# Downsampled and local attention feeding a SiLU layer: q and k on the two partition halves, 18 transposes for each early pair, later landings in the planner, paced loads

## The chip, the cores and the metric

The kernel runs on one core of a Trainium2 chip. The metric is the device time in microseconds (us) of one execution. Engines are named as in the profile: PE is the matmul engine (PEld its weight loads), DVE, ACT and POOL are the vector, scalar and GpSimd engines, SP issues DMAs.

## The reference, cut to what matters

Inputs are q, k and v of shape 8 x 8 x 576 x 64 (batch, heads, sequence, head width) and two weight matrices, 512 x 2048 and 2048 x 512, all float32.

```python
def _attn_ref(q, k, v):
    q_d = q.reshape(B, H, Sd, 4, D).mean(axis=3)      # k_d, v_d likewise, Sd = 144
    out_up = np.repeat(sm_attn(q_d, k_d, v_d), 4, axis=2)
    mask = np.abs(pos[:, None] - pos[None, :]) < 4
    scores = np.where(mask, scale * np.matmul(q, k.transpose(0, 1, 3, 2)), -1e9)
    ...
    return out_up + np.matmul(attn, v)                # attn: softmax of scores

x = attn_out.transpose(0, 2, 1, 3).reshape(B * S, H * D)   # 4608 x 512
h = x @ w_in                                               # 4608 x 2048
out = (h * (1.0 / (1.0 + np.exp(-h)))) @ w_out             # 4608 x 512
```

So there are two attentions for each head, one over sequence elements averaged by four and one in a band of seven, whose sum is the input of a two-layer network.

## The kernel before, in words

Two heads make a pair; there are 32 pairs, four to a batch. For a pair p the stages are:

- **Loads** (`load_qk`, `load_v`, `load_vq`): q and k go into one of four buffers `qk`, v into `vs` (four 64-partition DMAs) and, from pair 14 on, into `vq`. SP issues nearly all of them (L464 is the helper that issues every DMA). A partition of `qk` holds nine sequence rows of one head. The q load fills 128 partitions with both heads of pair p. The k load starts one head later, so it holds the second head of pair p and the first head of pair p+1; the first head of pair 0 is fetched alone, through `Rb`, by `lkx` and cast by `ckx`.
- **Casts** (`cast`, L535 to L544; `castw`, L551 and L554; `castv`): to bf16, on DVE and ACT for pairs 0 and 1 and on POOL later. `qkb` has NB = 3 buffers.
- **Transposes** (`pe_T`, L572): 36 of 64 x 64 for a pair, q into the PSUM bank `o0` and k into `pe_`, in an order that visits the four quadrants of the PE array in turn. `after_T` evacuates them to `qT` (L362) and `kT` (L582) and sums groups of four into `qd` and `kd` (L586, L590, and L597/L599 on POOL for pairs 0 to 7).
- **S** (`pe_S`): banded and downsampled scores into the banks `AB`; `after_S` takes exponentials on ACT (L624, L626) and applies the band mask on DVE (L628).
- **Z and PV** (`pe_main`): softmax sums and the products with v, into `CD` (for pairs 1 and 3 into `HP`). The reciprocals are spread over `Rb`, for pairs 0 to 9 by ten matmuls (`RB`, L735; the three-part split of the reciprocal is L707 to L714) and later through a DRAM scratch.
- `after_PV` multiplies (L745) and POOL adds the two attentions into `xT` (L769).
- **g1 and g2**: the first layer runs in 144 groups of four float32r matmuls into one of two `HP` banks, then tanh on ACT (L783) and a product on DVE into `gT` (L785). The second layer runs in 144 groups of four bf16 matmuls into `o0` or `pe_`; ACT evacuates (L800) and SP stores. L359 is the helper that issues all matmuls except transposes.

The program is written as units with a guessed cost each. Pairs 0 to 9 have separate units T, S, Z, PV, RB and VP; groups of g1 come in from the sixth round. From pair 10 on one unit V holds S of pair n, the transposes of pair n+1 and the rest of earlier pairs, with four g1 and four g2 parts written behind it. `feed` creates the loads and casts as far ahead as the buffers allow. `Plan.order` then simulates the five engines with the guessed costs and landing times, picks for each engine the ready unit of best priority inside a window (14 for PE), and so fixes the order of every engine's stream. At run time each engine follows that order and waits on semaphores. `tick` can make the loads of a pair wait for the exponentials of an earlier pair, from pair NTH on; with NTH = 99 it never acts. The weights (`load_w`) come in eight 1 MiB reads that POOL issues, with planned times from 16 us on.

Of the kernel before, what the change touches and what calls it, by code (L numbers as in the profile page):

```python
# [18 lines left out]
NVP = 14  # L19
NDIR = 10  # L20
NEQ = 12
NTH = 99
NMQ = 8


# [126 lines left out]
class Unit:  # L152


    __slots__ = ("eng", "name", "ops", "cost", "dcost", "prio", "idx", "pre", "succ", "npre",
                 "ready", "start", "end", "fifo")

    def __init__(self, eng, name, cost, prio, dcost=0.0):
        self.eng, self.name, self.cost, self.prio, self.dcost = eng, name, cost, prio, dcost
        self.ops, self.pre, self.succ = [], set(), []  # L160
        self.ready = 0.0


FIRST = {
# [2 lines left out]
class Plan:  # L167
# [50 lines left out]
    def order(self, look, first):  # L218

        todo = {e: first.get(e, "").split() for e in Prog.ENGS}  # L220
        free = {e: 0.0 for e in Prog.ENGS}
        ring = {e: 0.0 for e in Prog.ENGS}
        for u in self.units:
            u.pre = {v for v in u.pre}
            u.npre = len(u.pre)
            for v in u.pre:
                v.succ.append(u)
        pend = {e: [u for u in self.units if u.eng == e] for e in Prog.ENGS}
        head = {e: 0 for e in Prog.ENGS}
        taken = set()  # L230
        res = []
        left = len(self.units)
        while left:
            best = None
            for e in Prog.ENGS:
                lst = pend[e]
                while head[e] < len(lst) and lst[head[e]] in taken:
                    head[e] += 1
                if todo[e]:
                    win = [next(u for u in lst[head[e]:] if u.name == todo[e][0] and u not in taken)]  # L240
                    if win[0].npre:
                        continue
                else:
                    win = [u for u in lst[head[e]:head[e] + look[e]] if u not in taken and not u.npre]
                if not win:
                    continue
                t = max(free[e], min(u.ready for u in win))
                c = min((u for u in win if u.ready <= t + 0.05), key=lambda u: (u.ready - 100000 if u.fifo else u.prio, u.idx))
                t = max(t, c.ready)
                if best is None or t < best[0]:  # L250
                    best = (t, c)
            t, u = best
            del todo[u.eng][:1]
            u.start = t
            free[u.eng] = t + u.cost
            if u.dcost:
                e = u.eng
                begin = max(t + u.cost + 0.4, ring[e])
                other = max(x for y, x in ring.items() if y != e)
                ring[e] = begin + u.dcost + min(u.dcost, max(0.0, other - begin))  # L260
                u.end = ring[e] + (3.2 if e == "ACT" else 1.6)
                if e == "SP":
                    free[e] = max(free[e], ring[e] - 4.0)
            else:
                u.end = t + u.cost + self.LAT[u.eng]
            for v in u.succ:
                v.npre -= 1
                same = v.eng == u.eng and not u.dcost
                v.ready = max(v.ready, t + u.cost + (0.06 if u.eng != "PE" else 0.0) if same else u.end)
            taken.add(u)  # L270
            res.append(u)
            left -= 1
        res.sort(key=lambda u: u.start)
        return res


def bass_hourglass_attn__then__act_silu_kernel(
# [9 lines left out]
    with kctx:  # L287
        E = kctx.enter_context
        L = Plan()
# [20 lines left out]
        vs = sb("vs", [128, 10, 64], F32, NVS)  # L310
        vq = sb("vq", [128, 4, 256], F32, NVQ)
        vt = sb("vt", [128, 4, 128], F32)
        qkb = sb("qkb", [128, 2, 576], BF16, NB)
        vb = sb("vb", [128, 10, 64], BF16, NV)
        vd = sb("vd", [128, 4, 64], BF16, NV)
        qT = sb("qT", [128, S_], BF16, NT)
# [144 lines left out]


        def dma(eng, name, out_, in_, w, sem, dcost, r=(), prio=None, cost=0.42):
            return one(eng, name, cost, lambda s: s.dma_start(out_, in_), r, w, sem, prio, dcost)  # L464

        def tick(p, d):
            return [R(f"tick{p - d}")] if p >= NTH else []

        def load_qk(p):
            i = p % NQK  # L470
            ek = "ACT" if p < 1 else "SP"
            if p == 0:
                dma("ACT", "lkx", Rb[NR - 1][64:128, 0:576], bass.AP(tensor=k.tensor, offset=k.offset,
                                                                   ap=[[576, 64], [1, 576]]),
                    [R(f"Rb{NR - 1}1")], "kx", 0.5, prio=-20)
            dma("SP", f"lq{p}", qk[i][:, 0, :], bass.AP(tensor=q.tensor, offset=q.offset + 128 * p * 576,
                                                        ap=[[576, 128], [1, 576]]),
                [R(f"qk{i}0")], f"qk{i}0", 0.85, r=tick(p, 4), prio=10 * p)
            n = 128 if p < NPAIR - 1 else 64
            dma(ek, f"lk{p}", qk[i][0:n, 1, :], bass.AP(tensor=k.tensor, offset=k.offset + (128 * p + 64) * 576,  # L480
                                                          ap=[[576, n], [1, 576]]),
                [R(f"qk{i}1")], f"qk{i}1", 0.85, r=tick(p, 4), prio=10 * p)

        def load_v(p):
            i = p % NVS
# [45 lines left out]

        def cast(p):
            i, j = p % NQK, p % NB
            if p == 0:
                one("ACT", "ckx", 0.7, lambda e: e.activation(qkb[NB - 1][64:128, 1, :], Rb[NR - 1][64:128, 0:576],  # L535
                                                              AF.Copy),
                    r=[R(f"Rb{NR - 1}1")], w=[R(f"qkb{NB - 1}1")])
            if p < 2:
                one("DVE", f"cq{p}", 0.45, lambda e: e.tensor_copy(qkb[j][:, 0, :], qk[i][:, 0, :]),  # L539
                    r=[R(f"qk{i}0")], w=[R(f"qkb{j}0")])  # L540
                one("DVE", f"ck{p}", 0.45, lambda e: e.tensor_copy(qkb[j][:, 1, :], qk[i][:, 1, :]),  # L541
                    r=[R(f"qk{i}1")], w=[R(f"qkb{j}1")])
            else:
                one("POOL", f"c{p}", 1.15, lambda g: g.tensor_copy(qkb[j][:, :, :], qk[i][:, :, :]),  # L544
                    r=[R(f"qk{i}0"), R(f"qk{i}1")], w=[R(f"qkb{j}0"), R(f"qkb{j}1")])

        def castw(p):
            i, m = p % NVS, p % NV
# [14 lines left out]

        def pe_T(u, p):
            a, b = p % NB, (p - 1) % NB
            for r in range(9):
                for j, h, x, t, n in ((0, 0, 0, o0, a), (0, 1, 1, pe_, a), (1, 1, 0, o0, a), (1, 0, 1, pe_, b)):
                    o = t[half(h), 0:288].bitcast(BF16)[:, 64 * r:64 * r + 64]  # L570
                    w = qkb[n][half(j), x, 64 * r:64 * r + 64]
                    L.op(u, lambda e, o=o, w=w, j=j: e.transpose(o, w, idn[half(j), :]),  # L572
                         [R("id"), R(f"qkb{n}{x}")], [rE if x else rF])

        def after_T(p):
            j = p % NT
# [230 lines left out]
        def T(p):  # L807
            made.add(("T", p))
            u = L.unit("PE", f"T{p}", 0.45 if p > 1 else 0.9)
            pe_T(u, p)  # L810
            after_T(p)

        def VP(p):
# [42 lines left out]
        def feed():  # L856

            for p in range(NPAIR):
                for name, fn, need in (
                    ("lqk", load_qk, ("c", NQK)), ("c", cast, ("T", NB - 1)),  # L860
                    ("lv", load_v, ("cw", NVS)), ("cw", castw, ("PV", NV)),
                    ("lvq", load_vq, ("cv", NVQ)), ("cv", castv, ("PV", NV)),
                ):
                    src = {"c": "lqk", "cw": "lv", "cv": "lvq"}.get(name)
                    if p < NVP and name in ("lvq", "cv"):
                        made.add((name, p))
                    if (name, p) in made or (src and (src, p) not in made):
                        continue
                    if p >= NTH and name[0] == "l" and ("x", p - (4 if name == "lqk" else 3)) not in made:
                        continue  # L870
                    if p >= need[1] and (need[0], p - need[1]) not in made:
                        continue
                    if name in ("lv", "lvq") and ("lqk", p) not in made:
                        continue
                    made.add((name, p))
                    fn(p)
# [42 lines left out]
        while todo or todo2:  # L919
            if n < NPAIR + 2:  # L920
# [3 lines left out]
                if n <= NVP:  # L924
                    VP(n - 1)
                feed()
            m = 4
            G1(1 if m else 0)
            G2((0,))
            G1(1 if m else 0)  # L930
            G2((1,))
            G1(1 if m else 0)
            G2((2, 3))
            G1(m - 3 if m else 0)
            n += 1
        P = Prog()
        for u in L.order({"PE": 14, "ACT": 40, "DVE": 40, "POOL": 30, "SP": 40}, FIRST):
# [36 lines left out]
```

## Time and profile before

| | |
|---|---|
| median of 4 runs (lowest to highest) | 359.89 us (358.64 to 359.96) |
| the profiled execution: its own time, its span | 359.96 us, 358.2 us |
| PE busy | 331.3 us, 4742 matmuls |
| DVE, ACT, POOL busy | 222.5, 182.0, 156.2 us |
| matmuls of the first layer (HP) | 576, 162.6 us |
| matmuls of the second layer (o and pe_) | 576, 133.8 us |
| transposes (L572) | 1152, 33.6 us |
| moved by DMA | 60.28 MB, mean 168 GB/s |

Busy times of matmuls overlap each other and themselves, so they don't add to the span. In lines of the profile, a row gives the line of the kernel, the engine, the operation, output<-input, shapes and count, then busy us, mean ns, and the engine's idle time just ahead of such instructions with what released it. "issue" is time in which an engine waited for nothing that the profile shows.

### The profile page before, as it was taken

To read this page: it belongs to the slowest core of one execution; us is meant where nothing else is said; L and a number is where in the kernel's file an instruction comes from. 1 tells how busy PE (TensorE), PEld (TensorE's weight loads), DVE (VectorE), ACT (ScalarE), POOL (GpSimd) and SP (SyncE) were. 2 spreads that over 40 slices of the span, in tenths; PEclk is the share of its full clock that TensorE was granted. 3 is DMA by queue.
4 is the path that set the end of the run, shared out by engine and by line. 5 is a ranking of instruction groups with operands and counts; after the bars stand their busy time and mean duration, and the time that the engine had idled before them with its cause. 6 is when DMAs were issued, how large, how long until landed. Compare 5 with 4: busy or idle time off the path is not lost.

```text
span 358.2 us, 11023 instructions
## 1 busy us (share of the span) xinstructions
PE 331.3 (92%) x4742; PEld 214.6 (60%) x4742; DVE 222.5 (62%) x392; ACT 182.0 (51%) x326; POOL 156.2 (44%) x203
## 2 busy tenths in 40 slices
PE   0675599989999999999999999999999999999996
PEld 0454476667666666666666666666665565666642
DVE  7579659985666677777777767666655434343400
ACT  2855567875555555455545555555553444444421
POOL 7849774553455566655555657563111100000000
PEclk9996579999999999999999999999999999999999
DMA  8999999997998878877778775232032000110012
GB/s 234 239 277 277 292 274 238 267 228 208 234 284 235 228 218 214 233 203 225 212 226 211 215 196 161 73 119 75 33 123 95 31 29 29 42 48 29 31 59 88
DMA packets 73506, 60.28 MB, mean 168 GB/s; under 512 B 47986, under 2 KB 55794, under 8 KB 73458
## 3 DMA queue, kind: packets, MB, share of 16 engines
q1 hardware_dynamic: 63818, 44.27, 45.7%
q10 hardware_dynamic: 5416, 9.02, 8.8%
q0 software_dynamic: 4224, 6.29, 7.9%
q8 instruction: 37, 0.61, 0.7%
q14 instruction: 11, 0.09, 0.1%
HBM read 51.76 MB, written 9.91 MB: 172 GB/s over the span
## 4 chain that ended last, share of the span: by engine, by line
PE 87%; DVE 3%; SPq 2%; ACT 2%; issue 2%; POOL 1%; DMA 1%; ACTq 0%; POOLq 0%
PE HP L359 39%; PE o L359 28%; PE pe_ L359 8%; PE CD L359 6%; PE AB L359 4%; SPq L464 2%; PE o L572 2%; DMA vs<-in_v_dram 1%; DVE zr L707 1%; DVE rp L713 1%; DVE kd L586 1%; DVE rrest L711 1%; ACT Pt L624 0%; PE pe_ L572 0%; POOL w_in_sb L464 0%
## 5 line engine op out<-in xcount | busy, mean ns | idle before, releaser
L359 PE MATMUL HP<-xT,w_in_sb 128*128 128x512 f32 x576 | 162.6, 419 | 0.6 <-issue 0.5
L785 DVE SCALAR_TENSOR_TENSOR gT<-th,HP 128x512 bf16<-128x512 f32 x144 | 96.5, 683 | 101.4 <-ACT th L783 100.8
L783 ACT ACTIVATE th<-HP 128x512 f32<-128x512 f32 x144 | 86.1, 598 | 76.5 <-PE HP L359 74.3
L359 PEld LDWEIGHTS HP<-xT,w_in_sb 128*128 128x128 f32 x576 | 106.3, 190 | 27.3 <-issue 0.8
L359 PE MATMUL o<-w_out_bf,gT 128*128 128x512 bf16 x464 | 107.4, 380 | 0.1
L359 PEld LDWEIGHTS o<-w_out_bf,gT 128*128 128x128 bf16 x464 | 42.4, 98 | 54.9 <-issue 9.7
L769 POOL TENSOR_TENSOR xT<-xo 128x576 fp32r<-128x576 f32 (+3 forms) x48 | 44.1, 930 | 54.4 <-DVE xo L745 54.4
L800 ACT ACTIVATE osb<-o 128x512 f32<-128x512 f32 x29 | 17.3, 597 | 60.9 <-PE o L359 60.9
L554 POOL CAST vb<-vs 128x640 bf16<-128x640 f32 x30 | 21.8, 728 | 54.2 <-PE CD L359 41.9
L544 POOL CAST qkb<-qk 128x1152 bf16<-128x1152 f32 x30 | 34.3, 1145 | 5.4 <-DMA qk<-in_k_dram 4.6
L745 DVE TENSOR_TENSOR xo<-CD,Rb 128x720 f32<-128x720 f32 x30 | 27.0, 900 | 3.0 <-PE CD L359 1.1
L359 PE MATMUL pe_<-w_out_bf,gT 128*128 128x512 bf16 x112 | 26.4, 380 | 0.0
L559 POOL TENSOR_TENSOR vt<-vq 128x512 f32<-128x512 f32 x18 | 22.9, 1273 | 7.1 <-DMA vq<-in_v_dram 7.1
L572 PE MATMUL o<-idn,qkb 64*64 64x64 bf16 x576 | 17.2, 203 | 9.1 <-DVE qkb L539 6.3
L586 DVE TENSOR_REDUCE kd<-kT 128x144 bf16<-128x576 bf16 x32 | 23.3, 731 | 0.9 <-ACT kT L582 0.8
L582 ACT ACTIVATE kT<-pe_ 128x576 bf16<-128x576 bf16 x32 | 20.9, 654 | 1.7 <-PE pe_ L572 0.2
L624 ACT ACTIVATE Pt<-AB 128x576 bf16<-128x576 f32 x32 | 20.7, 647 | 1.5 <-PE AB L359 1.5
L572 PEld LDWEIGHTS o<-idn,qkb 64*64 64x64 bf16 x576 | 13.9, 118 | 11.0 <-DVE qkb L539 6.3
L572 PE MATMUL pe_<-idn,qkb 64*64 64x64 bf16 x576 | 16.4, 203 | 2.5 <-DVE qkb L541 1.9
L359 PEld LDWEIGHTS pe_<-w_out_bf,gT 128*128 128x128 bf16 x112 | 10.0, 98 | 13.6 <-issue 3.2
L590 DVE TENSOR_REDUCE qd<-qT 128x144 bf16<-128x576 bf16 x24 | 17.8, 744 | 0.0
L626 ACT ACTIVATE Pd<-AB 128x432 bf16<-128x432 f32 x32 | 16.9, 527 | 0.0
(79 smaller groups left out, 315.4 us busy)
## 6 DMA issues: line engine op xcount, KB each, us to landing
vs<-in_v_dram SPq DMA_DIRECT2D x126, 80.0 KB, 4.2
qk<-in_q_dram SPq DMA_DIRECT2D x32, 288.0 KB, 4.0
out_dram<-osb SPq DMA_DIRECT2D x36, 256.0 KB, 3.0
qk<-in_k_dram SPq DMA_DIRECT2D x30, 288.0 KB, 5.3
Rb<-scr ACTq DMA_DIRECT2D x44, 180.0 KB, 4.7
vq<-in_v_dram SPq DMA_DIRECT2D x18, 256.0 KB, 6.2
w_in_sb<-in_moe_w_in_dram POOLq DMA_DIRECT2D x4, 1024.0 KB, 9.4
w_out_bf<-in_moe_w_out_dram POOLq DMA_DIRECT2D x4, 512.0 KB, 9.3
```

The source lines that it names most:

```text
L359: L.op(u, lambda t: t.matmul(out_, lhsT, rhs, start=start, stop=stop, skip_group_check=True), r, w)
L544: one("POOL", f"c{p}", 1.15, lambda g: g.tensor_copy(qkb[j][:, :, :], qk[i][:, :, :]), r=[R(f"qk{i}0"), R(f"qk{i}1")], w=[R(f"qkb{j}0"), R ...
L554: one("POOL", f"cw{p}", 0.72, lambda g: g.tensor_copy(vb[m][:, :, :], vs[i][:, :, :]), r=rr, w=[R(f"vb{m}")])
L559: one("POOL", f"va{p}", 1.3, lambda g: g.tensor_tensor(vt[:, :, :], vq[i][:, :, 0:128], vq[i][:, :, 128:256], ALU.add), r=rr, w=[R("vt")])
L572: L.op(u, lambda e, o=o, w=w, j=j: e.transpose(o, w, idn[half(j), :]), [R("id"), R(f"qkb{n}{x}")], [rE if x else rF])
L582: one("ACT", f"ek{p}", 0.68, lambda e: e.activation(kT[j][:, 3:579].rearrange("p (g r) -> p g r", r=9), pe_[:, 0:288].bitcast(BF16).rearra ...
L586: one("DVE", f"mk{p}", 0.74, lambda e: e.tensor_reduce(kd[j][:, 0:SD], kT[j][:, 3:579].rearrange("p (g r) -> p g r", r=4), AX.X, ALU.add), ...
L624: one("ACT", f"x{p}", 0.66, lambda e: e.activation(Pt[m][:, :, :], AB[:, :, 0:288], AF.Exp, scale=0.125), r=rAB, w=[R(f"P{m}"), R(f"tick{p ...
L745: one("DVE", f"m{p}", 0.92, prio=-450000 if L.boost else None, r=rCD + [R(f"Rb{u}0"), R(f"Rb{u}1")], w=[R(f"xo{x}")], fn=lambda e: e.tenso ...
L769: one("POOL", f"a{p}", 0.15 + n * 0.0019, lambda g, dst=dst, in0=in0, in1=in1: g.tensor_tensor(dst, in0, in1, ALU.add), r=[R(f"xo{x}")], w ...
L783: one("ACT", f"t{j}_{f}", 0.62, lambda e: e.activation(th[tb][:, :], hps[hb], AF.Tanh, scale=0.5), r=[rH[hb]], w=[R(f"th{tb}")], prio=-1)
L785: one("DVE", f"s{j}_{f}", 0.71, lambda e: e.scalar_tensor_tensor(gT[j % 2][:, f, :], th[tb][:, :], 1.0, hps[hb], ALU.add, ALU.mult), r=[rH ...
```

## The change

- q of a pair goes to partitions 0-63 and k to partitions 64-127, both heads side by side in the free dimension; the separate fetch and cast of k's first head (`lkx`, `ckx`) disappear. The first k load stays on ACT's queue.
- `qkb` becomes [128, 9, 2, 64]: for each of the nine rows the two heads are neighbours. Casts write that order. Pair 0 is cast half on DVE, half on ACT; pair 1 in one DVE instruction; later pairs on POOL as before. A cast now needs the transposes three pairs back instead of two.
- `pe_T` takes a parameter. In the T units (pairs 0 to 10) it is wide: 18 transposes of 64 x 128. In V it stays at 36 of 64 x 64, in another order of quadrants.
- The planner assumes that SP loads with a priority number of 70 or more land 5.0 us after their transfer instead of 1.6. That is q and k from pair 7 on, `vs` from pair 6 on (later `vq` too).
- NTH is 12: from pair 12 on a q or k load waits for the exponentials of the pair four before, a v load for those of the pair three before.
- In the steady loop one g2 part is written first, then two g1, three g2 and two g1, instead of alternating.

```diff
-NTH = 99
+NTH = 12
+PLAT, LATE = 7, 5.0
...
-                u.end = ring[e] + (3.2 if e == "ACT" else 1.6)
+                u.end = ring[e] + u.lat
...
-        qkb = sb("qkb", [128, 2, 576], BF16, NB)
+        qkb = sb("qkb", [128, 9, 2, 64], BF16, NB)
...
+            u = one(eng, name, cost, lambda s: s.dma_start(out_, in_), r, w, sem, prio, dcost)
+            if eng == "SP" and prio is not None and prio >= 10 * PLAT:
+                u.lat = LATE
+            return u
...
+            for x, e, t in ((0, "SP", q), (1, ek, k)):
+                dma(e, f"l{'qk'[x]}{p}", qk[i][half(x), :, :],
+                    bass.AP(tensor=t.tensor, offset=t.offset + 2 * p * S_ * D_, ap=[[576, 64], [S_ * D_, 2], [1, 576]]),
+                    [R(f"qk{i}{x}")], f"qk{i}{x}", 0.85, r=tick(p, 4), prio=10 * p)
...
+            o, a = qkb[j][:, :, :, :].rearrange("p r h d -> p h r d"), qk[i][:, :, :].rearrange("p h (r d) -> p h r d", d=64)
+            rr = [R(f"qk{i}0"), R(f"qk{i}1")]
             if p == 0:
+                one("DVE", f"ca{p}", 0.45, lambda e: e.tensor_copy(o[:, 0], a[:, 0]), r=rr, w=[R(f"qkb{j}")])
+                one("ACT", f"cb{p}", 0.68, lambda e: e.activation(o[:, 1], a[:, 1], AF.Copy), r=rr, w=[R(f"qkb{j}")])
+            elif p < 2:
+                one("DVE", f"ca{p}", 0.85, lambda e: e.tensor_copy(o, a), r=rr, w=[R(f"qkb{j}")])
             else:
+                one("POOL", f"c{p}", 1.15, lambda g: g.tensor_copy(o, a), r=rr, w=[R(f"qkb{j}")])
...
-        def pe_T(u, p):
-            a, b = p % NB, (p - 1) % NB
+        def pe_T(u, p, wide=False):
+            b = p % NB
             for r in range(9):
-                for j, h, x, t, n in ((0, 0, 0, o0, a), (0, 1, 1, pe_, a), (1, 1, 0, o0, a), (1, 0, 1, pe_, b)):
-                    o = t[half(h), 0:288].bitcast(BF16)[:, 64 * r:64 * r + 64]
-                    w = qkb[n][half(j), x, 64 * r:64 * r + 64]
...
+                for h in range(1 if wide else 2):
+                    for x, t in ((0, o0), (1, pe_)):
+                        c = slice(0, 128) if wide else half(h)
+                        o = t[c, 0:288].bitcast(BF16)[:, 64 * r:64 * r + 64]
+                        w = qkb[b][half(x), r, :, :].rearrange("p h d -> p (h d)")[:, c]
...
-            pe_T(u, p)
+            pe_T(u, p, True)
...
-                    ("lqk", load_qk, ("c", NQK)), ("c", cast, ("T", NB - 1)),
+                    ("lqk", load_qk, ("c", NQK)), ("c", cast, ("T", NB)),
...
-            m = 4
-            G1(1 if m else 0)
             G2((0,))
-            G1(1 if m else 0)
-            G2((1,))
-            G1(1 if m else 0)
-            G2((2, 3))
-            G1(m - 3 if m else 0)
+            G1(2)
+            G2((1, 2, 3))
+            G1(2)
```

More of the change, by code (lines that the diff above doesn't have):

```diff
@@ L155 @@
     __slots__ = ("eng", "name", "ops", "cost", "dcost", "prio", "idx", "pre", "succ", "npre",
-                 "ready", "start", "end", "fifo")
+                 "ready", "start", "end", "fifo", "lat")
     def __init__(self, eng, name, cost, prio, dcost=0.0):
@@ L161, in __init__ @@
         self.ready = 0.0
+        self.lat = 3.2 if eng == "ACT" else 1.6
 FIRST = {
@@ L463, in dma @@
         def dma(eng, name, out_, in_, w, sem, dcost, r=(), prio=None, cost=0.42):
-            return one(eng, name, cost, lambda s: s.dma_start(out_, in_), r, w, sem, prio, dcost)
+            u = one(eng, name, cost, lambda s: s.dma_start(out_, in_), r, w, sem, prio, dcost)
+            if eng == "SP" and prio is not None and prio >= 10 * PLAT:
+                u.lat = LATE
+            return u
         def tick(p, d):
@@ L471, in load_qk @@
             ek = "ACT" if p < 1 else "SP"
[L472 to L482, printed above, removed]
+            for x, e, t in ((0, "SP", q), (1, ek, k)):
+                dma(e, f"l{'qk'[x]}{p}", qk[i][half(x), :, :],
+                    bass.AP(tensor=t.tensor, offset=t.offset + 2 * p * S_ * D_, ap=[[576, 64], [S_ * D_, 2], [1, 576]]),
+                    [R(f"qk{i}{x}")], f"qk{i}{x}", 0.85, r=tick(p, 4), prio=10 * p)
         def load_v(p):
@@ L533, in cast @@
             i, j = p % NQK, p % NB
+            o, a = qkb[j][:, :, :, :].rearrange("p r h d -> p h r d"), qk[i][:, :, :].rearrange("p h (r d) -> p h r d", d=64)
+            rr = [R(f"qk{i}0"), R(f"qk{i}1")]
             if p == 0:
[L535 to L542, printed above, removed]
-            else:
-                one("POOL", f"c{p}", 1.15, lambda g: g.tensor_copy(qkb[j][:, :, :], qk[i][:, :, :]),
-                    r=[R(f"qk{i}0"), R(f"qk{i}1")], w=[R(f"qkb{j}0"), R(f"qkb{j}1")])
+                one("DVE", f"ca{p}", 0.45, lambda e: e.tensor_copy(o[:, 0], a[:, 0]), r=rr, w=[R(f"qkb{j}")])
+                one("ACT", f"cb{p}", 0.68, lambda e: e.activation(o[:, 1], a[:, 1], AF.Copy), r=rr, w=[R(f"qkb{j}")])
+            elif p < 2:
+                one("DVE", f"ca{p}", 0.85, lambda e: e.tensor_copy(o, a), r=rr, w=[R(f"qkb{j}")])
+            else:
+                one("POOL", f"c{p}", 1.15, lambda g: g.tensor_copy(o, a), r=rr, w=[R(f"qkb{j}")])
         def castw(p):
@@ L562, in castv @@
                 vd[m][:, :, :], vt[:, :, 0:64], vt[:, :, 64:128], ALU.add), r=[R("vt")], w=[R(f"vd{m}0"), R(f"vd{m}1")])
-        def pe_T(u, p):
-            a, b = p % NB, (p - 1) % NB
+        def pe_T(u, p, wide=False):
+            b = p % NB
             for r in range(9):
-                for j, h, x, t, n in ((0, 0, 0, o0, a), (0, 1, 1, pe_, a), (1, 1, 0, o0, a), (1, 0, 1, pe_, b)):
-                    o = t[half(h), 0:288].bitcast(BF16)[:, 64 * r:64 * r + 64]
-                    w = qkb[n][half(j), x, 64 * r:64 * r + 64]
-                    L.op(u, lambda e, o=o, w=w, j=j: e.transpose(o, w, idn[half(j), :]),
-                         [R("id"), R(f"qkb{n}{x}")], [rE if x else rF])
+                for h in range(1 if wide else 2):
[3 more added lines that the diff above has]
+                        w = qkb[b][half(x), r, :, :].rearrange("p h d -> p (h d)")[:, c]
+                        L.op(u, lambda e, o=o, w=w, x=x: e.transpose(o, w, idn[half(x), :]),
+                             [R("id"), R(f"qkb{b}")], [rE if x else rF])
         def after_T(p):
```

## The prediction

> **What bounds the kernel now.** I read the strip of 40 slices first (each 8.96 us), with the DMA queue table.
>
> ```profile
> PE   0675599989999999999999999999999999999996
> ...
> PEclk9996579999999999999999999999999999999999
> DMA  8999999997998878877778775232032000110012
> ...
> q8 instruction: 37, 0.61, 0.7%
> ```
>
> PE is full from the ninth or tenth slice on, so from about 80 us the kernel is a queue of matmuls. Before that PE idles while the DMA engines are full, and in slices 4 to 6 it runs at about half clock. The windows view splits this:
>
> ```profile
> 50.00:60.00 10.00, 9.40 (x196) 6.57 (x189) 9.04 (x16) 8.57 (x17) 6.11 (x8) 1.00 1.16 248
> ...
> 120.00:140.00 20.00, 20.00 (x373) 13.34 (x371) 13.11 (x22) 11.02 (x20) 10.45 (x11) 1.00 0.81 219
> ```
>
> Columns: stretch, length, busy us and instructions of PE, PEld, DVE, ACT, POOL, clock, DMA share, GB/s. PE has no idle time in 120:140, nor in any stretch from 80 to 340. Idle PE is 358.2 - 331.3 = 26.9 us: 8.2 before the first transposes run (6.34 us of wait, 1.88 more), 3 at the end behind the last store, and some 15.7 in between, all before 80 us. The change can win only there, or lose anywhere.
>
> The waits view, PE alone, names part of it; the PE timeline shows where:
>
> ```profile
> PE HP L359 <- issue: 2.5, 2, 2.0
> PE AB L359 <- DVE rp L714: 2.4, 1, 2.4
> PE o L572 <- POOL qkb L544: 2.0, 3, 1.1
> ...
> PE CD L359 <- issue: 1.8, 1, 1.8
> ...
> PE AB L359 <- issue: 1.3, 1, 1.3
> ```
>
> ```profile
> 30.35 0.42 PE L359 MATMUL CD<-Pt,vb 64*64 64x58 bf16 x14 [1.83 <-issue]
> ...
> 37.64 0.36 PE L359 MATMUL HP<-Pt,vb 64*64 64x58 bf16 x9 [1.98 <-issue]
> ...
> 44.75 0.46 PE L359 MATMUL AB<-rp,gT 128*128 128x72 bf16 x5 [1.27 <-issue]
> ```
>
> Each stall cuts a run of equal matmuls in two: no operand is late. Three more windows count the matmuls between them:
>
> ```profile
> 30.30:37.60 7.30, 4.13 (x128) 3.39 (x128) 5.48 (x8) 3.46 (x7) 7.12 (x10) 0.50 1.31 289
> 37.60:44.70 7.10, 5.03 (x127) 4.12 (x128) 5.05 (x10) 3.79 (x8) 4.80 (x6) 0.50 1.27 308
> ```
>
> 128 matmuls with 128 weight loads are 256 instructions, and PE's 2 x 4742 instructions over 37 packets of queue q8 are 256.3 each. So PE waits for its own program: a block about every 7.2 us, behind a DMA system whose share is near 1.3. That costs 5.1 us (1.83 + 1.98 + 1.27).
>
> [...] In the trace four transposes start together (27.94, 27.95, 27.95, 27.95). [...]
>
> **The change part by part.**
>
> Wide transposes. 11 pairs x 18 = 198 matmuls and as many weight loads go, 1.55 blocks. By the third stall eight pairs have been transposed: 144 of 732 matmuls, so that point comes 1.1 blocks earlier in the program. Around it a pair has 123 matmuls (36 T, 28 S, 14 Z, 28 PV, 10 RB, 7 VP), then 105: a block lasts 123/105 = 1.17 times as long. The work inside the two stretches above, without their closing stall, is 7.3 - 1.98 = 5.3 and 7.1 - 1.27 = 5.8 us; times 1.17 it is 6.2 and 6.8, against 7.2 that a fetch needs. Stalls of 1.0 and 0.4 stay, say 0.6 for the first: 2.0 of 5.1, a gain of 3.1. Bounds: 0, if late loads fill the gap, and 5.1.
>
> Their own time. A narrow set took 0.54 us at half clock (40.78 to 41.32) and 0.31 at full (52.81 to 53.12). Of a wide transpose there is no row. Nearest are the ten RB matmuls of 128 x 128 with 72 columns: 0.71 us at half clock, 0.33 at full, 71 and 33 ns each. At 64 columns 18 of these are 1.14 or 0.53 us alone, half that if the two row groups overlap. So a wide set costs between 0 and 0.6 more at half clock; 8 such and 3 at full clock bound the sum at 5.4. [...] I take 0[...].
>
> First pair. `lkx` (144 KB) and `ckx` (0.68 on ACT) go; k of pair 0 is issued at 0.82 instead of 1.40 and has 0.6 us less in front (144 KB at 240 GB/s). T0 waits for the slower of the half casts (0.45 DVE, 0.68 ACT), so about 7.5 instead of 8.47. But the chain view goes at 8.74 to 12.90 through the v load of pair 1, behind SP's issues, and an ACT cast at 13.01; only the lighter queue helps it. I take 0.5, between 0 and 1.0.
>
> Casts. On POOL 1.15 us with another output order; POOL rows with three-dimensional patterns (L769, 1.22 for 576 elements) are no slower per element than plain ones (L559, 1.27 for 512), so 0; bound 0.5 x 8 pairs. DVE: 1.77 us becomes about 1.3. One pair more of room for `qkb` meets 2.0 us of PE waits on POOL casts; I take 0.5, as POOL is near full there (7.12 of 7.30).
>
> Later landings move only the planned order. POOL waited 9.3 us in five places for v before its cast, up to 2.3 each; at 42.08 that held back an `xT` addition (42.83) that HP needs. I take 0.4, between -1.5 (a cast put too late) and 1.5.
>
> Pacing adds a wait for ACT on SP from pair 12, behind which sit later loads and, from 84 us, stores. Pair 12 was loaded at 59.5 and now waits for its exponentials at about 63.5; its transposes come near 83. From there V takes 8.6 us: a load released by V(p-4) has three such rounds against a landing of 5 us. So 0; if SP stood still, `osb` has two buffers and ACT would stop after them.
>
> Steady loop: the planner already placed HP, HP, four g2, HP, HP after V, since `o0` holds transposed q until its copy is done; the new text gives the same. Narrow transposes keep four quadrants and 36 instructions. Tail unchanged: 0.
>
> New part: 3.1 + 0.5 + 0.5 + 0.4 = 4.5. Everything removed exposes the next limit: DMA share is 1.1 to 1.3 until 75 us, and loads pace POOL. I give back a quarter, 1.1, leaving 3.4. The profiled execution is 359.96 (span 358.2 and 1.8 around it), 0.07 above the median. **359.9 - 3.4 = 356.5 us.**
>
> **Rivals.** *The clock comes back earlier:* half clock ended at about 50, after the dense stretch that began at 45. HP work at half clock took 3.57 for eight matmuls against 1.85. [...]
>
> *DMA paces the start:* 8.76 MB moved from 20 to 50 us, and POOL waited for v right after. If all stalls turn into load waits, only the lighter queue, 0.5, is left: 359.4, no change.
>
> [...] each q or k load now fills 64 partitions. Rows to 64 partitions exist: 2880-byte packets into `Rb` have a median of 114 ns, 25 bytes per ns, like the 93 ns of 2304-byte q and k packets, but the upper quarter begins at 187 against 108. From 8 to 75 us there are 3137 q and k packets over 16 engines, 196 each. If a packet's mean rises by 50 ns (123 to 173), the loads need 9.8 us more; with the main gain gone too and two thirds of it exposed by full queues, 359.9 + 6.5 - 3.4 = 363.0. It decides from about 17 ns per packet, where 196 x 17 ns eats the gain.
>
> *Not what it says:* the order of the planner comes out worse (a cast waiting ahead of an addition) and wins nothing: 360 to 361, with the slower ones.
>
> **How the numbers follow.** Main case 0.42, early clock 0.16, DMA-paced 0.14[...]. About 0.3%, 1.1 us, is what a measurement of this kernel can tell from no change. Faster 0.42 + 0.16 = 0.58, same 0.14, slower 0.28. The main case alone spans 354 to 358; for 8 in 10 [...] 351 to 363. I predict 356.5.
>
> **What would show it.** Right: 4544 matmuls on PE, 35 or 36 q8 packets, "issue" waits under 2.5 us, HP starting before 45 us, PE full from under 80 us. Wrong: 2304-byte packets well over 123 ns and longer POOL waits on qk; wide sets over 0.8 us; PE idle after 80 us, with SP waiting for ACT Pt ahead of stores.

## The result, and the profile after

| | before | after |
|---|---|---|
| median over all runs (lowest to highest) | 359.84 us (358.08 to 363.08) | 362.06 us (359.86 to 365.67) |
| ratio, 95% interval | | 1.006 [1.0044, 1.0076] |
| the profiled execution: its own time, its span | 359.96, 358.2 | 362.02, 360.3 |
| PE busy, PE idle in the span | 331.3, 26.9 | 329.3, 31.0 |
| first HP matmul of the first layer | 45.0 us | 47.9 us |

Medians are over all executions; ratios and intervals leave out the few that took over 1.5% more than the fastest of their kernel.

The change made the kernel slower by 0.6%. I had forecast 356.5, faster. A rival of the prediction, slower packets for loads that fill 64 partitions, stood at 363.0. Below, "halves" are partitions 0-63 and 64-127, one for each q or k load as the change has it.

The strip and lines of the queue table of the changed kernel, and last the line of q1 before:

```profile
PE   0396499969999999999999999999999999999996
...
PEclk9997569999999999999999999999999999999999
DMA  8999999997989889998999999883212100100012
...
q1 hardware_dynamic: 63882, 44.42, 53.9%
...
q8 instruction: 35, 0.57, 0.7%
```

```profile
q1 hardware_dynamic: 63818, 44.27, 45.7%
```

The loss again lies before 80 us. Queue q1 is where to look first: its bytes are the same as before to 0.4% (44.42 against 44.27 MB), but its packets took 53.9% of 16 engines' span against 45.7%. The loads did not grow; their packets became slow. The windows of 8 to 50 us say it in one line for each kernel (stretch, length, busy us and instructions of PE, PEld, DVE, ACT and POOL, clock, DMA share, GB/s). Before:

```profile
8.00:50.00 42.00, 27.70 (x801) 21.94 (x802) 28.67 (x50) 24.59 (x48) 31.66 (x49) 0.76 1.15 273
```

After:

```profile
8.00:50.00 42.00, 26.25 (x626) 20.72 (x624) 25.27 (x48) 23.20 (x46) 30.55 (x46) 0.77 1.24 243
```

The engines' queues are fuller (1.24 against 1.15) and deliver less (243 against 273 GB/s). The trace's DMA records show which packets: from 8 to 75 us the 2304-byte packets of q and k have a mean of 157 ns, before 122. The waits view of POOL and PE (total us, times, longest), first two lines of before, then the changed kernel:

```profile
POOL vb L554 <- DMA vs<-in_v_dram: 9.3, 5, 2.3
...
POOL qkb L544 <- DMA qk<-in_k_dram: 4.6, 1, 4.6
```

```profile
POOL vb L549 <- DMA vs<-in_v_dram: 43.4, 21, 4.6
POOL qkb L540 <- DMA qk<-in_k_dram: 13.9, 14, 2.5
...
PE o L569 <- POOL qkb L540: 4.5, 3, 2.4
PE pe_ L569 <- issue: 2.8, 1, 2.8
PE HP L361 <- issue: 2.7, 1, 2.7
PE HP L361 <- POOL xT L766: 2.1, 1, 2.1
```

POOL's casts wait for k 14 times instead of once, and PE for POOL's casts 4.5 us instead of 2.0. The stalls on PE's own program, which the change was to shorten, are 5.5 us in two places, before 5.6 in four (the prediction's three and one of 0.5). The PE timeline shows them:

```profile
31.54 0.21 PE L569 MATMUL pe_<-idn,qkb 64*128 64x64 bf16 x1 [2.85 <-issue]
...
39.10 0.37 PE L361 MATMUL HP<-Pt,vb 64*64 64x58 bf16 x12 [2.66 <-issue]
```

The waits of POOL, and PE's wait for its casts, mislead: in experiment 7 a faster kernel has the same three. The two stalls, and the wait for `xT`, are gone there.

### The profile page after: what moved, and what is told of

Read it like the earlier page. It is cut to its first block, busy times and chain, and to the rows that moved or that the text cites. A ratio compares the mean times of both kernels' runs of the same rounds, so it can differ in the third digit from the quotient of the medians.

```text
span 360.3 us, 10635 instructions
## 1 busy us (share of the span) xinstructions
PE 329.3 (91%) x4544; PEld 215.4 (60%) x4544; DVE 222.2 (62%) x390; ACT 181.8 (50%) x326; POOL 158.2 (44%) x203
## 3 DMA queue, kind: packets, MB, share of 16 engines
q1 hardware_dynamic: 63882, 44.42, 53.9%
## 4 chain that ended last, share of the span: by engine, by line
PE 77%; DMA 12%; SPq 7%; POOL 2%; ACT 1%; issue 1%; DVE 0%; POOLq 0%; ACTq 0%
PE HP L361 34%; PE o L361 28%; DMA vs<-in_v_dram 9%; PE pe_ L361 7%; SPq L466 7%; PE CD L361 4%; DMA qk<-in_k_dram 2%; PE AB L361 2%; PE o L569 1%; POOL xT L766 1%; POOL vb L549 1%; PE pe_ L569 0%; POOL qkb L540 0%; DVE kd L583 0%; ACT vb L546 0%
## 5 line engine op out<-in xcount | busy, mean ns | idle before, releaser
L361 PE MATMUL HP<-xT,w_in_sb 128*128 128x512 f32 x576 | 157.3, 415 | 2.6 <-POOL xT L766 2.1
L361 PE MATMUL o<-w_out_bf,gT 128*128 128x512 bf16 x464 | 106.3, 380 | 0.0
L569 PE MATMUL o<-idn,qkb 64*64 64x64 bf16 (+1 forms) x477 | 16.6, 199 | 13.3 <-ACT qkb L536 7.9
L569 PEld LDWEIGHTS o<-idn,qkb 64*64 64x64 bf16 (+1 forms) x477 | 12.8, 109 | 17.6 <-DVE qkb L535 7.9
L569 PE MATMUL pe_<-idn,qkb 64*64 64x64 bf16 (+1 forms) x477 | 16.1, 199 | 3.6 <-issue 2.8
L625 DVE TENSOR_TENSOR Pt<-Pt,mask_bf 128x576 bf16<-128x576 bf16 x32 | 17.1, 535 | 1.9 <-ACT Pt L621 1.9
L361 PEld LDWEIGHTS pe_<-w_out_bf,gT 128*128 128x128 bf16 x112 | 10.1, 98 | 13.3 <-issue 2.7
```

The costliest lines, as they stand in the source:

```text
L361: L.op(u, lambda t: t.matmul(out_, lhsT, rhs, start=start, stop=stop, skip_group_check=True), r, w)
L569: L.op(u, lambda e, o=o, w=w, x=x: e.transpose(o, w, idn[half(x), :]), [R("id"), R(f"qkb{b}")], [rE if x else rF])
```

## The experiments

**Theory** after the result, P in the expectations: loads onto 64 adjacent partitions are slow (2304-byte packets of 157 ns against 122 above), and the rest of the change gains. Rivals: SP's longer issue; casts that come too late (`("T", NB)` and the wait for both loads); wide transposes that cost time; pacing that does harm. SP's issue is in the view of the line that issues DMAs (least, median and most ns), first before, then after:

```profile
L464 SPq DMA_DIRECT2D qk<-in_q_dram x32: 355/607/1996, 0.8 to 205.1; - x32
L464 SPq DMA_DIRECT2D qk<-in_k_dram x31: 424/433/1332, 1.7 to 205.7; - x31
```

```profile
L466 SPq DMA_DIRECT2D qk<-in_q_dram x32: 595/607/2802, 0.8 to 229.4; - x32
L466 SPq DMA_DIRECT2D qk<-in_k_dram x31: 599/608/1667, 2.2 to 230.0; - x31
```

Only the median of k rose, by 0.17 us for a pair; the q load had 0.61 before too.

**1. The layout alone, the planning alone.** The first is the change with `NTH = 99`, no later landings and the old loop; the second is the kernel before with exactly these three parts of the change. The first one's diff against the change begins:

```diff
-NTH = 12
-PLAT, LATE = 7, 5.0
+NTH = 99
...
```

> The changed kernel without its planning parts: no pacing, planned landings 1.6 us everywhere, the steady loop as before. Kept: q on partitions 0-63, k on 64-127, the casts, wide transposes for pairs 0 to 10. Theory P (each q or k load now fills 64 partitions[...], its packets slow down and the start, which waits for loads, stretches): slower than before by 1.5 to 4 us, 2304-byte packets from 8 to 50 us at about 160 ns mean as in the changed kernel (before 127). Theory O (the new planned order, later landings and pacing, costs the time): equal to before or up to 3 us faster, packets as they may be.

> The kernel before with the planning parts alone: pacing from pair 12, planned landings of 5.0 us, the new text of the steady loop. Loads, casts and transposes as before. Theory P: within 1 us of before, perhaps faster, 2304-byte packets at about 127 ns. Theory O: slower by about 2 us, with the waits of SP on ACT Pt seen in the changed kernel.

Layout alone: 370.59 us, 1.0301 [1.0255, 1.0347]. Planning alone: 358.5, 0.996 [0.9937, 0.9983]. So the layout costs some 10.8 us, far more than the whole change and than the 1.5 to 4 expected, and in the whole change the planning gives most of it back. In the layout alone the packets of q and k took 155 ns (8 to 75 us, before 122), and PE is no longer full after 80 us:

```profile
50.00:80.00 30.00, 27.38 (x467) 19.47 (x471) 26.46 (x46) 20.92 (x42) 17.91 (x22) 0.93 1.21 240
80.00:230.00 150.00, 146.16 (x2365) 95.56 (x2366) 101.86 (x165) 76.29 (x139) 84.85 (x98) 0.99 0.91 219
```

PE misses 3.8 of 150 us after 80, where the changed kernel misses 0.3 and the kernel before 0.1.

**2. Two halves against two parities, in the kernel before.** Each q or k load is cut in two, onto partitions 0-63 and 64-127 or onto even and odd ones. The two runs differ in `PARTS` alone, so in the partitions that a load fills and, with them, in the rows of DRAM that it reads (64 in a row, or every second one):

```diff
+PARTS = ((1, 0), (1, 64))
...
-            dma("SP", f"lq{p}", qk[i][:, 0, :], bass.AP(tensor=q.tensor, offset=q.offset + 128 * p * 576,
...
+            for y in range(2):
+                st, o = PARTS[y]
+                dma("SP", f"lq{p}", qk[i][o:(o + 64 if st == 1 else 128):st, 0, :],
...
```

For parities it is `PARTS = ((2, 0), (2, 1))`.

> The kernel before with every q and k load cut in two DMAs of 64 partitions, 0-63 and 64-127. Same bytes, packets, layout. Theory P: 2304-byte packets rise to about 160 ns from 8 to 50 us, and the time is 2 to 5 us above that of the run cut by parity. Rival I (what costs is SP's issue time[...], here 0.6 us for each more DMA): the same time as the run cut by parity, both slower than before by 1 to 3 us.

> As the run cut by halves, but the two DMAs of 64 partitions take the even and the odd partitions, so that each reaches both halves of the partitions. Instruction streams are the same but for the addresses. Theory P: packets near the 127 ns of before, time 2 to 5 us below the run cut by halves and near before, up to 2 us above it for SP's issues. Rival I: the same time as the run cut by halves.

Halves 371.99 (1.0349 [1.0302, 1.0395]), parities 368.95 (1.0268 [1.0219, 1.0316]); packets 139 against 126 ns. Which partitions a load fills is worth 3.0 us here at the medians (six executions each, 370.8 to 373.9 and 367.7 to 371.4). The other 9 us, where at most 2 were expected, come with the doubled number of loads: a pair's q and k took 0.607 + 0.433 us of SP at the medians and now take 2 x 0.617 + 2 x 0.597, 1.4 more. The planner also put the work of POOL and ACT in another order for them; which of the two costs the 9 us is not shown. This left the rival of SP's issue alive.

**3. Narrow transposes, casts one pair sooner, k loads on ACT's queue.**

```diff
-            pe_T(u, p, True)
+            pe_T(u, p)
...
-("c", cast, ("T", NB))
+("c", cast, ("T", NB - 1))
...
-            ek = "ACT" if p < 1 else "SP"
+            ek = "ACT" if p < 12 else "SP"
```

> The run with the layout alone (370.6), with all transposes narrow, 36 a pair also for pairs 0 to 10. Engine orders stay the same, since the planner's costs do not change. If wide transposes are part of the cost: 366 to 369. If they are free and the loads are the cost (theory P): 370 to 371. If they win through fewer program blocks, as forecast: 371.5 to 374.

> The run with the layout alone, but a cast is made only two transposes back, as in the kernel before, so the planner puts POOL's casts later. Theory C (the extra freedom lets POOL sit in a cast whose load is late: 13.7 us of POOL waits on qk from 8 to 100 us, against 4.6 before): 364 to 367, and those waits fall under 7 us. Theory P: 370 to 371, waits only move to others.

> The changed kernel with the k loads of pairs 0 to 11 issued by ACT instead of SP, so that a q load to partitions 0-63 and a k load to 64-127 are in flight at once and SP issues 11 DMAs less early. Theory P: 2304-byte packets of 20 to 50 us fall from 167 ns towards 130, time 358 to 361, below the changed kernel's 362.1, unless ACT's issue time (0.6 us each, 11 times) eats it. Theory O: no gain, 362 to 364.

The first two stand on the layout alone (370.59). Narrow: 372.47, 1.0353 [1.0305, 1.0401]. Its PE waits on "issue" are 10.2 us against 5.0 with wide transposes, so these halve the stalls, but the medians differ by 1.9 us only, the intervals overlap, and the two profiled executions, from which the stalls are read, took 370.84 and 371.08: less stall is not less time here. The other cast rule: 370.17, 1.0312 [1.0273, 1.0351]. POOL's waits on k fell from 13.7 to 6.6 us and those on v rose from 10.1 to 18.7: a POOL that waits for loads only changes which load it waits for. This rival falls: the time is the same. The third stands on the whole change and was a miss: 375.48, 1.0453 [1.0427, 1.048]. I wanted q and k in flight together on both halves, but the two engines went out of step (k of pair 4 was issued at 8.07 us on ACT, its q at 17.73 on SP), so packets stayed at 163 ns from 20 to 50 us (167 in the changed kernel) and PE waited 6.0 us in one place for an `xT` addition. It has no "issue" wait on PE at all, for all its slow packets. It says nothing on the halves.

**4. The change without pacing, and without later landings.**

```diff
-NTH = 12
+NTH = 99
```
```diff
-PLAT, LATE = 7, 5.0
+PLAT, LATE = 99, 5.0
```

> The changed kernel with NTH = 99, so that no load waits for an exponential. If pacing is what made up for the layout (loads of late pairs otherwise crowd out v and the weights around 60 to 80 us): 365 to 370. If the later planned landings did it: 361 to 363. If pacing costs: under 361.

> The changed kernel without the later landings. If pacing alone gives back what the planning gives in it: 361.5 to 363. If the landings share in it: 364 to 368, since the changed kernel without pacing took 368.4. Packets of q and k stay at 160 ns or more in 20 to 50 us in both.

Without pacing 368.38 (1.0256 [1.023, 1.0282]), without landings 366.58 (1.0172 [1.0136, 1.0207]). In the changed kernel pacing is worth 6.3 us and the landings 4.5; together, with the loop, 8.5. Neither does it alone.

**5. The same parts in the kernel before.**

> The kernel before with the later landings assumed from pair 7 on and the new order of the emission loop, without paced loads. Theory that pacing is what gained in the run of the planning alone (358.5): 359.5 to 360.5, within 0.2% of before. Theory that the assumed landings gained there: 358.0 to 358.8.

> The kernel before with paced loads and the new order of the emission loop, without later landings. Theory that pacing gained in the run of the planning alone: 358.0 to 358.8, first head-pair instruction at about 43.6 us. Theory that the landings gained: 359.5 to 360.5.

> The kernel before with the new order of the emission loop alone, without paced loads and without later landings. Both of those with this order took 358.0 and 358.6 one at a time, and 358.5 together. If the loop order made that gain: 357.8 to 358.8. If pacing or landings each make it: 359.4 to 360.4.

Landings and loop 358.02 (0.9967 [0.9942, 0.9991]), pacing and loop 358.57 (0.9954 [0.9929, 0.998]), loop alone 359.0 (0.9978 [0.9954, 1.0003]). All the intervals overlap, and that of the loop alone takes in no change: in the kernel before the planning is worth 0.2 to 0.5% and its parts can't be told apart. My expectations, one winner among the parts, were wrong. Each of the four planning versions has a lower median than the kernel before and after.

**6. The loads by themselves.** Eight loads of q and k at a time, 2.36 MB, after all other work of the kernel before, in one execution. Each group waits for the one before: full, halves in turn, parities in turn, four low then four high, full. The expected values begin with those of the theory.

```diff
+        def probe(g, dst, src, w):
+            P.op("SP", lambda e: e.dma_start(dst, src), r=last, w=w, dma=f"pr{g}")
...
+                if f == "full":
+                    probe(g, qk[b][:, x, :], rows(t, b, 128, 1, False), w)
+                elif f == "half":
+                    probe(g, qk[b][half(x), :, :], rows(t, b, 64, 1, True), w)
+                else:
+                    probe(g, qk[b][x:128:2, :, :], rows(t, b, 64, 1, True), w)
```

> The kernel before, with five groups of eight loads from q and k appended at its end, 288 KB each and 2.36 MB per group, one group at a time: two blocks onto all partitions (group 0 and again group 4), two 64-partition halves in turn with both blocks side by side (group 1, the form of the change), the same bytes onto even and odd partitions in turn (group 2), and four onto the lower half then four onto the upper (group 3). The added loads lengthen the run by some 40 to 50 us; only their records matter. [...] groups 0, 2 and 4 take about 6 us of data each (93 ns per 2304-byte packet, 400 GB/s over 16 engines), groups 1 and 3 longer, with packets over 110 ns; group 3, which never has both halves in flight, the longest, up to 10 us. Issue theory (the costs lie in SP's instruction of the 64x2x576 form alone): all groups have packets within 5 ns of one another; groups 1, 2 and 3 are issued at about 0.60 us each against about 0.40 for groups 0 and 4. Both can hold at once.

The windows from each group's first packet to the end of its last:

```profile
357.80:365.42 7.62, 0.00 (x0) 0.00 (x0) 0.00 (x0) 0.00 (x0) 0.00 (x0) 0.62 0.91 309
367.19:377.91 10.72, 0.00 (x0) 0.00 (x0) 0.00 (x0) 0.00 (x0) 0.00 (x0) 0.50 0.92 219
379.83:388.46 8.63, 0.00 (x0) 0.00 (x0) 0.00 (x0) 0.00 (x0) 0.00 (x0) 0.50 0.84 272
390.23:401.52 11.29, 0.00 (x0) 0.00 (x0) 0.00 (x0) 0.00 (x0) 0.00 (x0) 0.50 0.98 208
403.16:410.68 7.52, 0.00 (x0) 0.00 (x0) 0.00 (x0) 0.00 (x0) 0.00 (x0) 0.50 0.89 312
```

The last two columns count: the engines are about as full in all five, and move 309, 219, 272, 208 and 312 GB/s. Mean packets: 109, 154, 114, 172, 106 ns. The same bytes onto even and odd partitions come within 12 to 13% of the full form; onto halves the rate is 29 to 33% lower, whether the halves alternate or not. Halves and parities read the same rows of DRAM, so it is not the reading. Taking the halves in turn, 219 GB/s, is only 5% above one after the other, 208. Why the halves are slower is not shown. SP's timeline of the same run gives the issue (start, us):

```profile
359.02 0.43 SPq L943 DMA_DIRECT2D qk<-in_k_dram  x1
...
367.72 0.61 SPq L943 DMA_DIRECT2D qk<-in_k_dram  x1
...
380.37 0.61 SPq L943 DMA_DIRECT2D qk<-in_k_dram  x1
```

The form of 64 x 2 x 576 costs 0.61 us of SP on halves and parities alike, the full one 0.43 here. So both theories hold, and it had to be asked what each is worth in the kernel.

**7. The decision: only the partitions move.** The layout alone and the whole change, with q on even and k on odd partitions. Every engine's stream and the rows of DRAM that each load reads stay as they were, and the expected values again begin with those of the theory:

```diff
-                dma(e, f"l{'qk'[x]}{p}", qk[i][half(x), :, :],
+                dma(e, f"l{'qk'[x]}{p}", qk[i][x:128:2, :, :],
```

> The layout alone, with the same q and k loads aimed at the even (q) and odd (k) partitions in place of 0-63 and 64-127; every engine's stream is otherwise the same, and the values that meet on a partition are not those of the reference. It took 370.6 with halves. [...] packets of 2304 bytes fall from 164 to about 125 ns in 20 to 50 us, and at the 3.0 us per 18 ns of the split runs the time falls by some 6 to 7, to 363.5 to 365. Issue theory (SP's longer instruction, and casts that wait for both loads): packets may fall but the time stays at 368.5 to 371.

> The whole change with its q and k loads aimed at even and odd partitions, as in the run before; the values that meet on a partition are not those of the reference. It took 362.1 with halves. [...] 356.5 to 359, faster than the kernel before, so that the sign of the change hangs on where its loads land. Issue theory: 361 to 363.

Layout alone: 361.09, 1.0027 [1.0007, 1.0047], and 370.59 with halves. Whole change: 356.16, 0.9898 [0.9869, 0.9927], and 362.06 with halves. The executions of the two kinds don't overlap: 359.5 to 362.3 against 370.0 to 371.9, and 354.4 to 357.2 against 359.9 to 365.7. Where the loads land costs 9.5 us in the one and 5.9 in the other, enough to turn the sign. Both parity medians are below what the theory had expected (363.5 to 365, and 356.5 to 359). The runs show that the placement costs this time, not why. All else in the layout (SP's issue, joint waits, wide transposes) is worth +1.1 against the kernel before beside it. q1 of the layout alone, with halves and with parities:

```profile
q1 hardware_dynamic: 63882, 44.42, 51.1%
```

```profile
q1 hardware_dynamic: 63882, 44.42, 44.7%
```

The strip and q1 of the whole change with parities:

```profile
PE   0676799989999999999999999999999999999996
...
DMA  7899999956787988888998888972222000100012
...
q1 hardware_dynamic: 63882, 44.42, 47.6%
```

The same bytes as after, at 47.6% instead of 53.9%; in 20 to 50 us packets of 123 instead of 167 ns. Its waits view:

```profile
POOL vb L549 <- DMA vs<-in_v_dram: 43.9, 19, 3.6
POOL qkb L540 <- DMA qk<-in_k_dram: 15.1, 13, 2.4
...
PE o L569 <- POOL qkb L540: 4.6, 3, 2.3
...
PE o L361 <- issue: 0.3, 2, 0.2
...
PE pe_ L361 <- issue: 0.2, 1, 0.2
```

POOL waits as long for its loads as in the changed kernel, and PE as long for POOL's casts (4.6 us, there 4.5), in a run that is 5.9 us faster. So these waits are not what the halves cost; that on v comes with the pacing (without it, in experiment 4, 12.5 us). The stalls on PE's program are gone, 0.5 in three tiny pieces instead of 5.5, and the first HP matmul is at 43.7. These 5.0 us are about the difference of the two profiled spans, 360.3 and 355.4; PE's other waits moved by at most 1.9 each, up and down. So between these two runs the slow loads show on PE as stalls on its program, not as longer waits for operands. That the stalls themselves cost this time is not shown: in experiment 3 they halved without it.

The medians in one table (us; the kernel before ran at 358.98 to 359.95 beside them). Between the first two rows lies all of the layout but its halves, between the last two nothing but partitions. All of the planning is worth 1.3, 4.9 and 8.5 us in the three rows, so it depends on the rest of the layout too, not on slow loads alone:

| | no planning | landings, loop | pacing, loop | all three |
|---|---|---|---|---|
| kernel before | 359.84 | 358.02 | 358.57 | 358.5 |
| layout, parities | 361.09 | not run | not run | 356.16 |
| layout, halves | 370.59 | 368.38 | 366.58 | 362.06 |

The parity version is no kernel to use, since `pe_T` reads q from partitions 0-63 and k from 64-127. Of those that can be used, the kernel before with landings, pacing or both is the fastest, at 358.0 to 358.6.

## Why the prediction was wrong, step by step

**The step that failed** is the price of the loads in the main case: nothing, with slower packets put into a rival. The rival's own sum was near: it took 50 ns more per packet (measured 35 between before and after, and 40 between parities and halves), two thirds of it exposed, +6.5 (measured +5.9), against a gain of 3.4 (measured 3.7, 359.84 to 356.16), and so 363.0 for 362.06. In part that is luck. Its text says that the main gain is gone too, yet its sum keeps all of the 3.4. And no fixed share is exposed: 37 ns more over 196 packets, 7.3 us, cost 9.5 in the layout alone, and 40 ns, 7.9 us, cost 5.9 in the whole change. How much of the loads' time shows depended on the planning, which the prediction had put at 0.4. The point of decision, 17 ns, was far passed. What was wrong was the weight. I had seen 64-partition packets in the profile before, the 2880-byte ones into `Rb`, and weighed their median of 114 ns over their upper quarter at 187 (174 over all 2816 of them), when the quarter was nearer (172 ns in the fourth group above, where loads to one half follow one another). The row that I took to speak on it was read by its mild end.

**Program stalls, 5.1 to 2.0.** In the changed kernel 5.5, with parities 0.5. Wide transposes do reach further with each block of some 256 instructions (a pair has 105 matmuls where it had 123), but the step took 7.2 us between two fetches as fixed, and it is not: after the change the fetches on queue q8 come at 28.0, 36.2 and 44.7, 8.3 us apart, against 27.7, 34.9 and 41.8, 7.0 apart, before. Nor does the distance make the stall: with parities they come at 29.0, 38.2 and 47.2, 9.1 apart, and PE does not stall. A fetch itself took 1.1 to 1.7 us in these records, and each stall, before and after, ended 1.4 to 1.8 us after a fetch's record did, which fits the reading as a wait for the program; what decides when a fetch starts is not shown. The 5.1 was also one execution's: the probe run, whose first 355 us are the program of the kernel before, has 2.4 where that has 5.6. And the stall is not worth its size: in experiment 3, 5.2 us fewer of it gave 1.9 at the medians and none in the profiled executions.

**First pair.** Forecast: transposes at 7.5 instead of 8.47. Measured 7.89, and 7.28 with parities. Right, and the late 0.4 goes with the halves.

**Casts and wide sets.** POOL's cast has a median of 1142 ns, before 1143: 0 was right. A wide set at half clock (0.50 granted) took 0.66 us end to end (44.84 to its last start at 45.26 plus 0.24), a narrow one 0.78 (40.78 to 41.56, 0.50 too) in the kernel before. In the wide set the q and k transposes of a row start within 0.01 us of each other. 0 was right, and the bound of 5.4 was never near. The 0.5 for more room in `qkb` was not seen; PE's wait on POOL's casts rose from 2.0 to 4.5, and to 4.6 with parities, so the slow loads are not why.

**Later landings +0.4 and pacing 0.** Both too small in the changed kernel: 4.5 and 6.3, each beside the other. Without both, and with the old loop, PE loses 3.8 us after 80 us. I priced these parts in the kernel before, where they are worth 1.3 with the loop, not in the kernel that the rest of the change makes. That SP would wait for ACT's exponentials came true (36.9 us in 18 places); PE still misses only 0.3 of 150 us after 80.

**The clock.** That full clock would come back earlier, and what that would be worth, was my estimate. It came back later: 0.50 granted from 45 to 50 us and 0.88 from 50 to 55, before 0.51 and 1.00.

**The give-back of 1.1** stood for the loads. 356.16 with parities beside the forecast of 356.5 says that the sum without the slow halves was near, not that each term was: the layout without them lost 1.1 where it was to gain, and the planning then gained 4.9 where 0.4 was forecast. Of the signs named for being right, the 4544 matmuls and 35 packets came, but HP began at 47.9 and "issue" waits were 5.5; of those for being wrong, the packets well over 123 ns came.

What stays open: how the 1.1 us of the layout with parities divides between SP's longer issue and the stalls that vanish, why landings and pacing need each other, why the planning is worth 4.9 us in the layout with parities and 1.3 in the kernel before, and when PE stalls on its program: some runs with fast loads do, and three with slow or doubled loads do not.

## What to carry to other kernels

When a change puts the same bytes on 64 adjacent partitions, price every packet first at what such loads took here (154 to 172 ns for 2304 bytes, against 106 to 114) and ask whether the stage is bound by loads; only then count what the new layout saves. Here the upper quarter of a group of durations, not its median, stood for loads that follow one another; ask which case the new stage will be. Put a wait down to a cause only after looking whether it goes when the cause goes. Price an accompanying change (pacing, assumed landings) in the kernel that the other parts make, and test a suspected layout cost by moving the addresses alone.

## What I had not expected of the hardware

- In the probe, loads onto 64 adjacent partitions cost 40 to 66 ns more per 2304-byte packet when they follow one another (154 and 172 against 106 to 114 ns), and alternating the two halves repairs only 5% of the rate (219 against 208 GB/s).
- In the probe a load of 64 x 2 x 576 takes 0.61 us of SP's time and one of 128 x 576 0.43, for the same bytes; but in the kernel before, q loads of 128 x 576 had a median of 0.61 too, and k loads 0.43. Why is not shown. Twice as many loads, with the order planned for them, cost 9 us.
- PE's stalls on its own program are no fixed property of a kernel, and no run shows one cause of them. Sums of PE's "issue" waits in single executions: 5.0 to 10.2 us in six with q and k on halves (after, layout alone, narrow, late casts, without pacing, without landings), but none with the k loads on ACT, whose packets were as slow (169 ns from 8 to 75 us), and none in the two runs with loads cut in two. With fast packets it was 0 to 1.1 in four (planning alone, loop alone, both parity runs) and 5.2 to 5.6 in three (before, pacing and loop, landings and loop). The same program gave 5.6 in the run before and 2.4 in the probe run.
